# Eight shared 4 KB tiles as eight tags, handed out by the kernel, and another written order of tasks

## The chip, the cores and the metric

The kernel runs on one core of a Trainium2 chip. The metric is the time of one execution on the device, in microseconds (us), lower being better. The core has five engines that run side by side: TensorE (PE; its weight loads are listed as PEld), VectorE (DVE), ScalarE (ACT), GpSimd (POOL) and SyncE (SP), which here only starts transfers (DMAs). Each engine takes its instructions in the order in which the program gives them; semaphores between engines hold an instruction back until what it reads is there, or until a buffer that it writes is free.

## The reference

The reference is a DeltaNet attention (4 batches, 8 heads, 768 positions, head size 48) followed by a feed-forward layer with a cosine gate. Cut to what is computed:

```python
k_n = k / (norm(k) + 1e-06)
for t in range(S):                       # state: (B, H, D, D), zero at first
    y[:, :, t] = einsum('bhd,bhde->bhe', q[:, :, t], state)
    v_old = einsum('bhde,bhd->bhe', state, k_n[:, :, t])
    state = state + beta[t] * einsum('bhd,bhe->bhde', k_n[:, :, t], v[:, :, t] - v_old)
x = y.transpose(0, 2, 1, 3).reshape(3072, 384)
h = x @ w_in                             # (384, 2048)
out = (h * cos(h)) @ w_out               # (2048, 384)
```

## The kernel before

**Units and pairs.** The 768 positions are cut into 24 chunks of 32, the units n = 0 to 23, each for all 32 pairs of batch and head at once; two units make a pair m = n // 2. Within a unit the recurrence is solved as a triangular system, and between units a state is handed on, so the units follow each other.

**What a unit does.** SyncE loads its k, q and v (L308). In the first eight units TensorE turns k and q (task turn, L513) and ScalarE copies the result out (turn_out, L523). TensorE forms the products of keys and queries (gram, L544), and VectorE takes them out of PSUM as gram_keys (L555) and gram_queries (L578). The keys' norms come by way of square (ScalarE, L448), sum (VectorE, L453), norms (GpSimd, L465) and scale (VectorE, from L476). The two grams of a pair go to memory in the device (gram_put) and come back in another layout (gram_get, L609 and L617); the triangular matrix is inverted in pieces (inv, L654 and L661): on VectorE for pair 0, in four pieces, and on GpSimd for the others, in seven. The inverse goes out (put, L675) and comes back for each unit (get, L686 and L694). For unit 0 half of get's eight DMAs are started by ScalarE, the others by SyncE. Then TensorE runs state (L711), for units 0 and 1 solve_half, between (both L741) and solve (L774), for others solve alone, then update (L797) and within (L814). VectorE's right, between_out, solve_out (two instructions, L784) and update_out (L805) and ScalarE's half_out and within_out carry the values between them. The features (L833, L840) of two units are the 128-column input of the feed-forward layer of pair p.

**The feed-forward layer.** For p = 0 it is plain: hidden 0,f for eight even f (L884, three PSUM banks in turn), the gate as turns (ScalarE, L924), rest (VectorE, L931), cos (ScalarE, L940) and gate (VectorE, L943), and out 0,i,k (L1026). For p from 1 on the products are done by Strassen's scheme with seven products in place of eight (layer, L1001; the second matrix, L1083). Both weight matrices arrive as 64-bit words, in 28 loads of 512 KB (w_in, 0 to 11) or 384 KB (w_out, 12 to 27), each into a 4 KB tile (L413), and are narrowed by split (two instructions on ScalarE, L421 and L423), shift (two on VectorE, L427 and L432) and add (one on GpSimd, L436). The load is called weights t, and its steps split t, shift t and add t.

**What sets the order.** The work is a set of 1869 tasks, put in with `add` under names such as ("gram", 5), each with its dependencies and the tiles that it makes and uses. A text, `Order.LINE`, lists their indices in the order in which `run` emits them. Engines take their tasks in the order of that list; the tile framework puts in the semaphores. A task stands in the queue of its engine alone, so the list decides what is queued behind what.

**The shared tiles.** Eight tiles of 4 KB per partition have the tag "g". They hold, one after another, `bq`, `eye16` and `halves_z` (constants of the start), `t_beta`, the words of each weight load (`pairs`, free after add t), the squares of keys (`ksq`, free after sum), the half solutions of units 0 and 1 (`u_half`) and the gates (`g_ffn`, free after the last product that reads them). A task that makes such a tile waits, in its engine's queue, until the last user of the tile that it gets is done. PSUM gives one tile each to the tags "kq" and "two" (turned keys, grams, half solutions, updates, features), three to "h" and two halves to the output.

Of the kernel before, what the change touches and what calls it, by code (L numbers as in the profile page):

```python
# [10 lines left out]
FP = mybir.dt.float32  # L11
I32 = mybir.dt.int32
U32 = mybir.dt.uint32
# [3 lines left out]
C = 32  # L17
# [36 lines left out]
0 1 2 3 4 5 6 1757 72 10 37 14 11 7 12 42 38 1761 39 13 15 40 16 43 17 44 1758 18 45 46 19 75 73 20  # L54
48 1765 50 79 96 49 1769 97 47 76 1759 77 80 104 78 99 131 51 1762 81 105 52 53 54 1773 9 154 55
1777 82 100 56 1770 36 1766 1778 1763 1771 134 101 1760 102 106 107 1774 135 41 1781 1772 108 1767
83 136 22 1782 109 1783 23 1775 1764 132 84 1785 1779 21 1789 1784 110 1793 1786 1768 1780 1776 24
25 1787 185 111 26 27 1797 28 29 137 57 1801 30 32 31 1790 33 138 58 155 139 34 74 1788 35 112 1805
140 59 669 1794 1798 141 670 142 60 674 113 1791 1802 1806 61 1803 114 186 62 1799 143 63 115 1809
64 65 66 68 208 1813 671 116 67 98 158 1817 675 676 69 1804 86 239 677 117 1795 188 672 159 1792  # L60
1818 160 118 103 1814 161 1810 1821 87 119 679 162 1800 678 70 680 1819 133 681 1815 163 189 673
1825 1796 71 1811 192 684 682 1822 1823 85 1820 1807 683 1826 193 689 1816 190 164 1827 690 694 165
691 685 8 1808 1812 692 191 1824 1829 88 262 686 709 89 1828 90 166 92 693 1830 687 93 695 721 167
688 91 696 697 699 1833 1834 1831 94 704 156 95 194 168 700 1837 1835 121 157 120 195 698 196 1841
812 701 122 1832 241 705 702 1836 1838 1842 197 737 123 706 703 124 707 209 1845 169 293 242 742 125
708 738 739 722 1846 126 1843 1839 127 128 1849 710 170 129 743 740 130 1844 744 1840 187 747 171
741 745 752 212 1850 1847 172 1853 316 1851 746 748 1848 1857 757 213 749 753 754 214 755 750 1858
245 145 1854 756 762 751 173 215 1852 758 146 808 1855 759 763 216 1861 760 1859 217 711 1862 764
767 1856 1863 144 1860 243 1865 265 147 1864 761 1866 148 725 218 768 772 149 1867 1868 151 769 770
246 295 219 771 220 152 150 174 729 153 244 726 730 712 713 221 175 715 210 176 222 177 211 247 223  # L70
716 178 733 179 180 347 181 714 266 182 717 773 248 183 765 774 199 809 775 810 723 184 776 249 250
718 200 267 268 736 224 811 719 269 777 781 296 780 817 766 240 734 819 783 778 818 782 731 816 820
271 225 832 720 784 813 251 821 727 822 724 299 779 226 227 272 786 823 833 788 825 789 826 319 735
790 824 273 834 827 835 829 791 792 785 297 794 728 298 828 830 270 198 201 840 836 841 796 787 274
300 837 797 842 843 814 838 798 831 202 203 301 844 845 846 799 205 848 800 847 370 206 839 850 795
849 204 793 275 229 852 230 228 851 231 854 863 853 801 320 232 276 233 235 856 864 321 802 277 804
207 732 263 880 855 349 857 865 805 236 278 279 234 815 302 806 858 859 353 303 294 867 237 803 304
879 860 317 868 869 866 238 322 807 280 253 871 882 264 870 323 872 873 874 861 911 862 910 281 912
305 913 324 325 875 885 886 876 914 915 877 878 252 881 254 327 917 916 326 926 888 883 354 887 927
928 401 884 890 919 920 350 918 255 351 891 256 929 921 923 934 922 892 893 930 924 935 931 352 932  # L80
257 374 259 894 896 258 328 373 282 260 936 933 925 898 424 938 897 937 283 939 942 940 284 943 944
946 329 355 895 375 889 330 941 285 899 900 286 947 287 948 945 331 950 957 901 332 951 261 958 288
902 949 356 289 333 290 952 903 904 959 960 357 954 953 961 974 965 906 334 455 407 907 966 358 962
291 955 963 905 908 376 967 964 307 968 318 973 292 976 308 335 1005 956 979 359 980 408 306 969
1006 1004 403 970 1007 478 975 404 377 378 971 1009 972 309 982 409 310 1008 311 313 1020 405 379
909 977 428 984 336 380 978 312 985 381 1010 1021 986 314 987 337 988 990 1022 338 992 1011 993 1013
1014 1023 981 1012 406 1015 1016 1017 994 339 315 1028 1024 1029 340 983 995 1018 1019 382 1025 1026
989 1027 509 462 427 1030 341 348 1031 1032 383 996 342 384 997 1033 1036 998 991 1038 1034 1037 410
343 1068 1040 1000 411 344 1001 1039 385 1051 1052 457 1041 1053 1035 412 1042 386 1002 1043 1054
1067 1044 1046 1045 387 413 345 1047 461 999 429 1055 346 1070 1073 1048 1049 1059 1056 1060 1050  # L90
1061 1062 430 1057 361 1063 371 1099 1058 431 1064 1100 388 1003 1065 1098 1074 482 1101 1071 402
1103 1066 372 389 362 1102 433 1069 1076 360 1104 1105 1078 1079 1107 1072 1106 1114 1115 390 1077
435 1080 434 432 1116 1109 1081 363 1082 1084 364 458 463 365 367 1117 366 1108 1086 1111 436 1087
368 437 1122 1085 1088 532 1075 481 1123 1083 1110 1124 1118 1089 1125 1112 459 1119 391 1120 1090
1130 1121 369 425 392 393 1131 1113 1126 394 460 1127 438 456 1132 395 1091 396 516 1134 1128 1129
479 515 464 426 397 1092 1133 1136 398 439 440 1145 441 399 1135 1094 1095 1093 1137 1146 465 1096
466 1138 1140 1147 1161 400 1139 1141 1148 1142 563 1149 1097 1143 1164 1162 1150 442 480 1151 1152
1163 1153 1144 1167 1157 483 1193 1168 484 1158 415 1192 1159 1160 443 467 1170 1154 485 1155 1156
1172 1194 1195 1173 486 1196 487 1165 1197 1166 517 1199 414 511 1198 1208 416 586 536 1200 1174
1201 417 1175 1176 1178 418 1203 488 1169 512 1209 1180 513 1202 1204 1181 1212 489 1210 1182 1205  # L100
1213 419 490 1214 1171 421 570 1211 1216 1217 1183 1215 1206 1218 420 444 1219 514 535 422 1184 1224
1207 491 1225 1220 1177 1226 1227 1221 1228 1179 565 445 1185 1222 1223 423 446 447 1230 1186 492
448 537 1188 1189 1239 1229 1240 1231 617 493 1241 449 451 452 566 1232 1233 1190 1234 1236 1235 450
510 1256 1242 1243 1247 1255 1258 1237 569 518 469 1244 1248 1245 453 1246 1238 1187 454 590 1191
1249 494 1251 1261 1250 1262 1287 519 1252 1253 1288 1289 1286 1259 520 1254 470 1290 538 539 1302
1264 495 496 1291 567 1257 497 541 1260 1292 1293 1266 540 1295 1303 1294 521 1267 1296 1297 1304
1263 1298 571 1268 1306 1299 1305 1307 468 543 1308 1269 542 471 1270 1309 544 1272 640 1300 1318
472 498 533 1310 473 1311 1301 1265 545 589 475 1274 474 1312 1313 1314 1271 1275 546 476 623 619
1276 499 1277 1320 477 1319 1315 1278 500 1316 591 501 1279 1273 502 568 503 1317 547 504 564 1322
548 624 1280 1324 1321 1333 1323 534 1334 572 505 1282 1326 573 1350 1325 506 507 1283 1328 1327 574  # L110
1284 1329 1281 575 1330 549 592 1337 1335 1336 523 1331 1349 593 1341 508 1338 1342 620 550 1343
1339 1352 1340 1344 1332 1381 551 1355 1345 1346 595 643 1382 1356 621 1347 1383 1380 524 1385 522
1348 1353 1351 1387 1358 1386 1389 1384 622 1390 1388 1396 1360 594 587 1391 1354 1397 1361 525 1398
597 1393 526 527 1399 596 529 598 1392 1404 599 530 1405 1406 600 528 1400 1407 1362 1285 1394 1395
1363 601 553 1364 1357 1366 1412 625 1408 602 644 1359 1401 1368 1409 1402 552 1410 554 1369 1370
1411 618 531 555 1414 556 1413 1371 1403 1415 1416 1372 1418 557 645 1373 558 1367 1417 626 1419
1374 1427 559 1420 1365 627 560 1376 1428 1422 641 1429 628 603 1421 1377 1430 561 604 1375 1424 642
1378 562 1423 605 1443 1425 588 1431 1432 1426 1439 1446 1433 646 1440 1441 577 1434 1449 1442 1475
1379 1450 1435 1436 1476 1474 1452 647 1437 1438 648 1477 1447 1479 576 1481 1480 1454 1483 1444 578
1478 649 651 1445 1448 629 1451 1482 1484 1455 579 1456 580 1485 581 583 650 1457 1486 1458 1490  # L120
1494 1495 1491 582 652 584 1496 1460 1492 1493 1487 1498 607 1499 1497 585 1462 608 606 1488 1489
1461 1463 1459 1464 1502 1465 653 609 1466 1453 1506 1503 1504 654 1500 610 611 655 1501 613 1507
1467 1508 1468 1505 614 1510 1512 1470 1509 1521 1511 1522 1523 1471 612 1514 1515 1513 1524 1516
# [1454 lines left out]
```

## Time and profile before

| | |
|---|---|
| three runs | 670.10, 670.51, 671.60 us; median 670.51 |
| profiled execution | 673.52 us, of which the span of its instructions is 671.7 |
| mean granted clock of TensorE | 0.959 |
| busy: PE, DVE, ACT, POOL | 607.6, 466.9, 223.6, 343.5 us |
| share of the span | 90%, 70%, 33%, 51% |
| moved by DMA | 59.65 MB, mean 89 GB/s |

All times that carry a position ("at 88.3 us") count from the start of the span of the profiled execution. "Busy" is the time in which an engine works on instructions that the profile counts. "Idle before" is the time in which an engine stood still ahead of an instruction, and the releaser is the instruction or DMA whose end let it go on; where the profile finds none, it writes "issue". The granted clock is TensorE's, as a share of its full speed. The chain of waits follows the work back from the last instruction to whatever released it.

### The profile page before, as it was taken

What the parts mean: (1) busy time and instruction counts of PE and PEld (TensorE: products, weight loads), DVE (VectorE), ACT (ScalarE), POOL (GpSimd) and SP (SyncE); (2) the same over time, 40 slices, a digit from 0 to 9 for tenths busy, and PEclk for the clock granted to TensorE, in tenths of its full rate; (3) what the DMA queues carried; (4) which work ended last, traced back from release to release, by engine and by line L of the source; (5) the groups of instructions that cost most, each with busy time, mean ns of one, the idle gap of its engine ahead of it and who ended that gap; (6) DMA issues with size and microseconds to landing.
All of it is one profiled execution on the core that took longest, in us unless ns stands there. A gap on an engine that the chain in (4) does not pass through costs nothing.

```text
span 671.7 us, 27640 instructions
## 1 busy us (share of the span) xinstructions
PE 607.6 (90%) x12060; PEld 571.4 (85%) x12060; DVE 466.9 (70%) x912; ACT 223.6 (33%) x376; POOL 343.5 (51%) x734
## 2 busy tenths in 40 slices
PE   3326669999899999999999999999999999999997
PEld 3215668886698999999999999999989999999997
DVE  6783548856887786858777877768776766656662
ACT  3342255543132332323423333333322324323330
POOL 4278748876878358318448358368284084000000
PEclk9556969999999999999999999999999999999999
DMA  7886564475464553554555354454623213001001
GB/s 164 200 193 153 115 148 103 99 147 99 83 113 79 106 94 62 90 98 69 113 93 96 68 96 81 74 85 94 112 47 79 55 23 87 6 21 53 1 13 35
DMA packets 237084, 59.65 MB, mean 89 GB/s; under 512 B 228516, under 2 KB 231860, under 8 KB 236964
## 3 DMA queue, kind: packets, MB, share of 16 engines
q1 hardware_dynamic: 233956, 57.03, 42.9%
q8 instruction: 94, 1.54, 1.0%
q10 hardware_dynamic: 2752, 0.43, 0.4%
q0 software_dynamic: 256, 0.44, 0.3%
q14 instruction: 26, 0.21, 0.1%
HBM read 43.17 MB, written 14.68 MB: 86 GB/s over the span
## 4 chain that ended last, share of the span: by engine, by line
PE 83%; DMA 4%; DVE 3%; issue 3%; POOL 3%; SPq 3%; ACT 1%; ACTq 0%; DVEq 0%; POOLq 0%
PE p_h L1001 29%; PE p_out L1083 29%; PE p_h L884 6%; PE p_kq L711 4%; PE p_s L797 3%; PE p_u L774 3%; PE p_kq L814 3%; PE p_out L1026 2%; PE p_g L544 2%; PE p_o L1083 2%; SPq L308 1%; DMA qp<-in_q_dram 1%; POOL knrm L465 1%; DMA x_ffn<-y_dr 1%; POOL z L661 1%
## 5 line engine op out<-in xcount | busy, mean ns | idle before, releaser
L654 POOL TENSOR_TENSOR part<-z,gb 128x126 f32<-128x126 f32 (+22 forms) x341 | 133.2, 391 | 107.9 <-DMA gb<-g_dr 52.6
L661 POOL TENSOR_TENSOR z<-z,part 128x126 f32<-128x126 f32 (+22 forms) x341 | 137.7, 404 | 26.7
L1001 PE MATMUL p_h<-x_ffn,w_in 128*128 128x128 f32 x1120 | 143.2, 276 | 0.7 <-issue 0.7
L1001 PEld LDWEIGHTS p_h<-x_ffn,w_in 128*128 128x128 f32 x1120 | 135.4, 192 | 1.9 <-issue 0.9
L1083 PE MATMUL p_out<-w_out,g_ffn 128*128 128x192 f32 x672 | 122.1, 329 | 0.0
L924 ACT ACTIVATE turns<-p_h,quarter_turn 128x512 int32<-128x512 f32 x96 | 65.2, 685 | 149.6 <-DVE p_h L1019 101.0
L1083 PEld LDWEIGHTS p_out<-w_out,g_ffn 128*128 128x128 f32 x672 | 107.7, 190 | 1.5
L940 ACT ACTIVATE turns<-turns,halfpi 128x512 f32<-128x512 f32 x96 | 68.0, 720 | 90.7 <-DVE turns L931 90.3
L1083 PE MATMUL p_out<-w_sum,g_ffn 128*128 128x192 f32 x496 | 88.7, 329 | 0.0
L931 DVE SCALAR_TENSOR_TENSOR turns<-p_h,turns 128x512 f32<-128x512 f32 x96 | 65.1, 682 | 28.6 <-ACT turns L924 28.3
L1083 PEld LDWEIGHTS p_out<-w_sum,g_ffn 128*128 128x128 f32 x496 | 79.7, 190 | 1.0
L943 DVE TENSOR_TENSOR g_ffn<-turns,p_h 128x512 f32<-128x512 f32 x96 | 64.7, 679 | 14.4 <-ACT turns L940 12.1
L465 POOL TENSOR_TENSOR knrm<-ksum,halves 128x16 f32<-128x16 f32 (+1 forms) x14 | 36.4, 2605 | 64.2 <-DVE ksum L453 52.7
L1016 ACT COPY g_ffn<-p_h 128x512 f32<-128x512 f32 x60 | 34.9, 582 | 97.3 <-PE p_h L1001 97.2
L1099 DVE TENSOR_TENSOR g_ffn<-g_ffn 128x512 f32<-128x512 f32 x88 | 61.5, 708 | 1.7 <-PE p_out L1083 1.6
L1019 DVE TENSOR_TENSOR p_h<-g_ffn,p_h 128x512 f32<-128x512 f32 x60 | 41.4, 691 | 30.2 <-PE p_h L1001 24.1
L884 PE MATMUL p_h<-x_ffn,w_in 128*128 128x128 f32 x384 | 48.5, 286 | 1.2 <-DVE g_ffn L943 0.8
L1133 DVE SCALAR_TENSOR_TENSOR o<-p_out,o 128x192 f32<-128x192 f32 x74 | 25.1, 351 | 33.8 <-PE p_out L1083 30.3
L884 PEld LDWEIGHTS p_h<-x_ffn,w_in 128*128 128x128 f32 x384 | 46.5, 200 | 2.3 <-DVE g_ffn L943 0.9
L1001 PE MATMUL p_h<-x_sum,in_sum 128*128 128x128 f32 x320 | 41.6, 277 | 0.0
L784 DVE TENSOR_TENSOR u<-p_u,bz 128x384 f32<-128x384 f32 x48 | 24.4, 549 | 21.8 <-PE p_u L774 21.8
L1001 PEld LDWEIGHTS p_h<-x_sum,in_sum 128*128 128x128 f32 x320 | 38.8, 192 | 0.6
(111 smaller groups left out, 728.9 us busy)
## 6 DMA issues: line engine op xcount, KB each, us to landing
pairs<-in_moe_w_in_dram SPq DMA_DIRECT2D x12, 512.0 KB
pairs<-in_moe_w_out_dram SPq DMA_DIRECT2D x16, 384.0 KB
gb<-g_dr SPq DMA_DIRECT2D x22, 256.0 KB
vp<-in_v_dram SPq DMA_DIRECT2D x96, 48.0 KB
out_dram<-o SPq DMA_DIRECT2D x23, 192.0 KB
y_dr<-y SPq DMA_DIRECT2D x20, 192.0 KB
x_ffn<-y_dr SPq DMA_DIRECT2D x40, 96.0 KB
kp<-in_k_dram SPq DMA_DIRECT2D x128, 24.0 KB
```

The costliest lines, as they stand in the source:

```text
L465: nc.gpsimd.tensor_tensor(out=scales[m][2][:, part], in0=sums[m, part.start][:, 0:n], in1=halves[:, 0:n], op=ALU.pow,)
L654: eng.tensor_tensor(out=part, in0=z[:, 0:rows, j, None].to_broadcast(shape), in1=a[:, j, None, j + 1 :].to_broadcast(shape), op=ALU.mult,)
L661: eng.tensor_tensor(out=behind, in0=behind, in1=part, op=ALU.subtract)
L884: nc.tensor.matmul(p_h[:, i], w_in[:, t, (4 * k + i) * 128 : (4 * k + i + 1) * 128], moved(p, t, unit), start=(t == 0), stop=(t == KT - 1),)
L924: nc.scalar.activation(turns[p, f], hidden_of(p, f), AF.Identity, bias=quarter_turn, scale=TURN)
L931: nc.vector.scalar_tensor_tensor(out=r, in0=hidden_of(p, f), scalar=TURN, in1=t, op0=ALU.mult, op1=ALU.subtract,)
L940: nc.scalar.activation(r, r, AF.Sin, bias=halfpi, scale=2.0 * math.pi)
L943: nc.vector.tensor_tensor(out=place(p, f), in0=step_of(rests.pop((p, f)), f), in1=step_of(hidden_of(p, f), f), op=ALU.mult,)
L1001: nc.tensor.matmul(p_h[:, e], in_sum[:, odd_tile, 4 * s + e] if a == "s" else w_in[:, a, f * 128 : (f + 1) * 128], x_sums[p][:, unit] if b ...
L1019: nc.vector.tensor_tensor(out=block(p, s, 0, 1) if i == 3 else p_h, in0=block(p, s, *one), in1=p_h, op=ALU.add,)
L1083: nc.tensor.matmul(p_o, left(p, part, a)[:, e % 4], right(e, b), start=(e == 0), stop=(e == FT // 2 - 1), skip_group_check=True,)
L1099: nc.vector.tensor_tensor(out=left(p, s, to), in0=left(p, s, one), in1=left(p, s, two), op=op)
```

## The change

The tag "g" of eight tiles becomes eight tags g0 to g7 of one tile each. `run` keeps a list of the free ones: a task that makes such a tile takes the first of that list, and the tag comes back at its end when the last user of the tile has been emitted. So the choice of the tile is made by the written list and not by the framework. The three constants take g0, g1 and g2. As a gate tile must be taken by the task that makes it, gate (p, f) for f = 2, 6, 10, 14 now also depends on gate (p, f - 2). The list `LINE` is a new one throughout: the same 1869 tasks, in another order.

```diff
     LINE = """
-0 1 2 3 4 5 6 1757 72 10 37 14 11 7 12 42 38 1761 39 13 15 40 16 43 17 44 1758 18 45 46 19 75 73 20
...
+0 1 2 3 4 5 6 1757 10 72 14 11 12 7 42 15 73 37 38 1761 39 13 16 43 75 17 1758 1762 40 18 76 44 45
...
     def run(self, wrote):
         keys, done = list(self.tasks), set()
         live, left = dict.fromkeys(self.bufs, 0), dict(self.users)
+        homes, free = {}, [f"g{i}" for i in range(self.bufs["g"])]
...
-            for tag, _ in makes:
+            for tag, t in makes:
                 live[tag] += 1
                 assert live[tag] <= self.bufs[tag], key
+                if tag == "g":
+                    self.home = homes[t] = free.pop(0)
             emit()
...
                 if left[t] == 0:
                     live[self.tiles[t]] -= 1
+                    if t in homes:
+                        free.append(homes[t])
...
-    bq = ffn_pool.tile([128, NU, C], FP, name="bq", tag="g", bufs=GATES)
+    bq = ffn_pool.tile([128, NU, C], FP, name="bq", tag="g0", bufs=1)
...
-        pairs = ffn_pool.tile([128, 4, TOK], U32, name="pairs", tag="g", bufs=GATES)
+        pairs = ffn_pool.tile([128, 4, TOK], U32, name="pairs", tag=order.home, bufs=1)
...
-            [128, 2, H, D], FP, name="ksq", tag="g", bufs=GATES
+            [128, 2, H, D], FP, name="ksq", tag=order.home, bufs=1
...
-        add(("gate", *key), "DVE", 0.73, lambda: hidden_gate(p, f), [("cos", *key)],
+        deps = [("cos", *key)]
+        if f in range(2, FT, 4):
+            deps.append(("gate", p, f - 2))
+        add(("gate", *key), "DVE", 0.73, lambda: hidden_gate(p, f), deps,
             makes=makes, uses=uses + [("turns", *key)], due=due)
```

The same replacement of the tag is made for `eye16`, `halves_z`, `t_beta`, `u_half` and `g_ffn`. Around the steps that the prediction speaks of, the new list stands against the old one so:

| engine | before | after |
|---|---|---|
| SP | weights 4, v 0, k 5, weights 5, put 0, v 1, weights 6, gram_put 3, q 4, gram_put 2, weights 7, get 0 | weights 4, k 5, weights 5, v 0, put 0, weights 6, gram_put 2, gram_put 3, v 1, weights 7, get 0 |
| ACT, early | inv_out 0, split 3, 2, 5, square 2,0, split 4, 6, half of get 0, split 7, half_out 0 | split 4, 3, inv_out 0, split 5, 2, square 2,0, split 7, half of get 0, split 6, half_out 0 |
| ACT, later | half_out 1, turns 0,2, within_out 1, cos 0,2, square 3,0, cos 0,0, turn_out 5 | turns 0,0, square 3,0, split 11, half_out 1, turns 0,2, turn_out 5, split 12, within_out 1, cos 0,0 |
| PE | update 1, within 1, turn 5, state 2, gram 5, hidden 0,4, features 1, turn 6, hidden 0,6, 0,8, 0,10, solve 2, out 0,0,0 | update 1, turn 5, within 1, gram 5, hidden 0,4, features 1, state 2, hidden 0,6, 0,8, turn 6, out 0,0,0, hidden 0,10, solve 2 |
| POOL | inv 1,4, add 11, inv 1,5, add 8, inv 1,6, add 10, add 9, add 15 | inv 1,2, add 8, inv 1,3, add 10, inv 1,4, add 9, inv 1,5, inv 1,6, add 11, add 15 |

## The prediction, made before the changed kernel ran

> **What bounds the kernel now.** I read the page's rows of busy tenths and of the granted clock first, then TensorE's waits before and after 100 us, then the chain of waits, and last the timelines of ScalarE, GpSimd and VectorE around the longest wait. From the page, the 40 slices (16.8 us each):
>
> ```profile
> PE   3326669999899999999999999999999999999997
> ...
> PEclk9556969999999999999999999999999999999999
> ```
>
> TensorE is 90% busy over the span, and from the seventh slice on nearly all the time. A new order can gain only in the first 180 us. There, of the first 100 us, are these waits of TensorE (engine, line, what it waited for: total, times, longest):
>
> ```profile
> PE p_w L741 <- DMA halves_z<-z_dr: 16.1, 1, 16.1
> ...
> PE p_g L544 <- ACT kq_t L523: 4.7, 1, 4.7
> ...
> PE p_kq L711 <- issue: 2.3, 1, 2.3
> ...
> PE p_t L513 <- ACT x_ffn L840: 0.8, 1, 0.8
> ```
>
> I summed all of TensorE's idle stretches over 0.25 us: 59.2 us, of which 41.2 lie before 76 us (loads, and the inverse of pair 0 that must come back through get 0), 10.1 between 76 and 109 us, 4.2 more up to 180 us, and 3.7 in single "issue" gaps after it. After 180 us no task waits for another engine: nothing is to be had there, only lost.
>
> The 4.7 us row is the wait of gram 5, at 83.61 to 88.34 us. The chain of waits shows how it came about (start, us, engine, operation):
>
> ```profile
> 84.57 1.29 POOL w_in L436
> ...
> 85.88 0.84 ACT ksq L448
> 86.72 0.61 ACT turns L940
> 87.33 0.96 ACT kq_t L523 x2
> ...
> 88.34 1.18 PE p_g L544 x61
> 89.53 5.43 PE p_h L884 x24
> ```
>
> ScalarE stood still in front of square 3,0 (its timeline):
>
> ```profile
> 85.88 0.84 ACT L448 ACTIVATE ksq<-kp 128x768 f32<-128x768 f32 x1 [5.82 <-POOL w_in L436]
> ```
>
> Square 3,0 needed a 4 KB tile, and the one it got was that of load 10, whose last user is add 10; add 10 stands on GpSimd behind the last piece of inverse 1 (78.37 to 84.61). Behind square 3,0 on ScalarE stood turn_out 5, for which gram 5 waited. The windows (us, then busy of PE, PEld, DVE, ACT, POOL, the granted clock, DMA share, GB/s) show what followed:
>
> ```profile
> 80.00:85.00 5.00, 1.35 (x128) 1.08 (x109) 0.93 (x1) 0.06 (x1) 4.14 (x13) 0.96 0.51 122
> 85.00:90.00 5.00, 1.66 (x66) 1.49 (x67) 0.44 (x2) 4.12 (x9) 2.09 (x2) 0.50 0.64 133
> 90.00:95.00 5.00, 5.00 (x26) 5.00 (x25) 2.12 (x5) 0.97 (x4) 1.01 (x1) 0.52 0.78 160
> ```
>
> The granted clock fell to half from 84.58 to 94.82 us, and hidden 0,4, which takes 2.85 to 2.95 us at full clock, took 5.49.
>
> **The change, part by part.** *Homes.* Eight tags of one tile in place of one tag of eight: no instruction is added. A tile now waits for the one tile whose last user stands earliest in the list among those free. By itself that is worth about 0: in the trace the tiles were handed out nearly in that order already. The added dependency of a gate on the gate two before it holds in both lists. What counts is the new list.
>
> *Start to 66 us: -0.5 us (-2 to +2).* Solve_half 0 waits 16.12 us for get 0, whose last DMA landed at 45.92. The inverse of pair 0 on VectorE carries scale 1,0 between its pieces now (five small instructions, 1.0 us) and ends about 31.3 us, not 29.9. Put 0 stands on SyncE behind loads k 5, weights 5 and v 0, where before v 0 came earlier; v 1 has moved behind weights 6 and two gram_puts. The four DMAs of q 4 no longer stand between put 0 and get 0. Against that: get 0 has half of its DMAs on ScalarE, now behind both instructions of split 7, which wait for weights 7. Issued about 36.8 us by the shorter queue, and with the 4.0 to 4.1 us that weights 5, 6 and 7 took to land, weights 7 is there at 41; that half is then issued at 41 to 43.5 and lands 1.5 to 2.5 us later (its rows), at 43 to 45. SyncE's half landed at 45.2 to 45.9, so it stays the later one, slightly earlier than before. If weights 7 isn't issued until after v 1's four DMAs, as late as before (41.04), its split ends at 46.5 and solve_half 0 comes 2 us late: the upper end. Behind it on ScalarE waits half_out 0, which needs solve_half 0 anyway.
>
> *76 to 109 us: -6.0 us (-7.7 to -4).* On ScalarE, turn_out 5 now stands behind square 3,0, as before, but square 3,0 comes earlier and its tile is that of load 6, whose add 6 ended long before 66 us; on GpSimd, add 10 has moved three pieces of inverse 1 ahead. So gram 5 no longer waits: -4.73. TensorE's list is now update 1, turn 5, within 1, gram 5, hidden 0,4, state 2, and so on, so matmuls fill 78 to 95 us and the clock should hold: hidden 0,4 takes 2.9 instead of 5.49, -2.6. The wait of turn 6 for features_out 1 (0.81) goes, for hidden 0,6 and 0,8 come before it. Removed: 8.1 us.
>
> Added: turn 5 needs the bank that update_out 1 gives back, right behind update 1: about 1.1 us, between the hand-overs of the same bank in this chain (0.74 and 0.75 ahead of solve 0 and 1, 0.93 ahead of between 0, 1.24 ahead of update 1). TensorE's whole queue stands behind it. Features 1 needs a bank from gram_queries 5, which stands on VectorE behind shift 12 and 14: 0.35 (two instructions of 0.55 and 0.35 there, less 0.5 of cover by hidden 0,4). Hidden 0,6 waits for gate 0,0 (one of three banks), and 0,8 for gate 0,2 behind features_out 1 and shift 13: 0.25 and 0.4. Sum 2.1; 8.1 - 2.1 = 6.0. The 2.26 us "issue" gap in state 2 has no releaser in the trace; I leave it where it is (if it came of the idle time, -1.7 more: the lower end). As a check, the list up to out 0,0,0 and hidden 0,10 holds the same matmuls in both; before it ends at 108.1, and durations at full clock added up along the new list with these waits end it at 101.8. Inverse 1 has add 8, 10 and 9 ahead of its last piece (before: 11 and 8), some 1.3 us more, so put 1 goes out at about 86 and get 2 lands, 12 us after put 1's issue as in the trace (84.64 to 96.73), at 98; solve 2 comes at 101: 3 us of cover.
>
> *109 to 180 us: -0.8 us (-1.5 to +0.5).* Update 5's wait of 1.53 goes (solve_out 5 stood behind weigh 3 and turn_out 8 on VectorE; weigh 3 is far later now). Update 2 gets 0.7, behind shift 18 and gate 0,8.
>
> *After 180 us: +1.2 us (0 to +4).* Two places. Six pairs of solve and update now have only one half product (1.31 us) between them, to cover solve_out's two instructions (2 x 0.549): a spare of 0.29 each, and VectorE finds something ahead of it about as often as not; 0.5 in all. And the loop of pair 8: gram_put 17 to solve 16 took 60.6 us in the trace (376.6 to 438.1 with gram 17's end), with 58.8 us of TensorE's work beside it. The new list has 48.6 us there. But gram_get 8 has moved up on SyncE, no longer behind get 14, k 21 and blocks 19,1, and get 16 stands right behind put 8: I shorten the loop by 10.7 us, to 49.9, and count 0.7.
>
> Sum: -0.5 - 6.0 - 0.8 + 1.2 = -6.1. The profiled execution took 673.52 (span 671.7 and 1.8 around it), so 667.4; the median of the three runs is 3.0 lower, 670.51, so **664.4 us**. With the stages' ends, not all at once, 660.5 to 667.
>
> **Rivals.** *The clock falls all the same (0.13): 668.* VectorE's chain over 82 to 92 us is dense now (shifts, gates, rests), and it runs beside GpSimd's adds. The same shift took (VectorE's timeline)
>
> ```profile
> 40.17 1.51 DVE L432 TENSOR_SCALAR w_in<-w_in 128x512 uint32<-128x512 uint32 x1
> ...
> 42.54 0.41 DVE L432 TENSOR_SCALAR w_in<-w_in 128x512 uint32<-128x512 uint32 x1
> ```
>
> the first beside an add, the second alone. Three such stretches ahead of gate 0,0 and 0,2 cost 3 x 1.1 = 3.3 us, for which hidden 0,6 and 0,8 wait; with a little of the half-clock time (2.6 at most) I take 3.5, and of the 6 us 2.5 are left. For it: the rows. Against it: of GpSimd's adds, 15, 12, 14 and 13 wait for shifts of this stretch, and 8, 9 and 10 are done by then. [...]
>
> *Nothing changes (0.08): 670.5.* The tiles come in the old order, square 3,0 waits for another late user, and the chain moves with it. The list speaks against it: add 6 stands a long way ahead.
>
> *Slower (0.17): 674.* The loop of pair 8 doesn't shrink. GpSimd's inverse 8 (396.2 to 424.5) is the same 28.3 us, so all must come from the time between gram_put 17 and inverse 8, 12 us of queueing and transfer in the trace. If it stays 12, solve 16 waits 60.6 - 48.6 = 12 us less what little else is brought forward, about 10: 664.4 - 0.7 + 10 = 674. It decides from half: once that stretch stays over 6 us, the gain at 76 to 109 us is spent. For it: the list gives the loop 10 us less of TensorE's work than before. Against it: the order on SyncE.
>
> **How the numbers follow.** The forecast has 0.62, the rivals 0.13, 0.08 and 0.17. What the measurement can tell from no change is about 0.2%, 1.3 us. Faster: 0.59 of the forecast and 0.10 of the clock's rival, 0.69. Same: 0.02, 0.02 and 0.06, 0.10. Slower: 0.21. The range of 660 to 672 takes in the forecast's own, the clock and no change, and leaves out the loop's case and the lowest ends, about 0.2.
>
> **What would show it.** ScalarE has no wait for an add ahead of square 3,0; gram 5 starts about 81 and not at 88.3; the clock stays 1.0 over 80 to 95 us; hidden 0,6 starts about 89 and not at 97.0; solve_half 0 starts between 44 and 46; update 5 has no wait. I'm wrong if TensorE has a wait of several us for get 16 near 430 us, for get 0 after 46, or for gates at 85 to 95.

## The result, and the profile after

The changed kernel takes 674.38 us (median of nine runs, 672.64 to 678.86 without one disturbed run of 684.0), the kernel before on the same chip 671.22. The ratio is 1.0056, with a 95% interval of 1.0030 to 1.0082: **0.56% slower**, where 664.4 us and 1% faster had been forecast, and outside the range. The profiled execution took 678.22 us (span 676.4), 4 us more than the median; a second profiled execution (the first experiment) took 675.52.

From the page of the changed kernel, the same two rows as of before:

```profile
PE   3308789989999899999999999999999999999996
PEclk9756899999989999999999998999999999999999
```

The stretch from 84 to 101 us (sixth slice) is 8 tenths busy where it had been 6. New are the 8s far behind, at slices 12 and 25 of the clock. The waits of TensorE (line, what it waited for, total, times, longest), in the kernel before behind 100 us:

```profile
PE p_kq L711 <- issue: 3.4, 3, 1.4
PE p_s L797 <- DVE u L784: 1.5, 1, 1.5
PE p_u L774 <- issue: 1.0, 1, 1.0
PE p_h L884 <- DVE g_ffn L943: 0.8, 1, 0.8
```

and in the changed kernel, first up to 76 us, then behind 100 us:

```profile
PE p_w L746 <- DMA halves_z<-z_dr: 24.1, 3, 23.0
```

```profile
PE p_kq L716 <- issue: 3.0, 2, 2.2
PE p_u L779 <- DMA zt<-z_dr: 2.6, 5, 1.1
PE p_out L1088 <- DVE g_ffn L1104: 2.4, 1, 2.4
PE p_h L889 <- DVE g_ffn L948: 1.6, 1, 1.6
PE p_out L1088 <- issue: 1.5, 1, 1.5
```

Gram 5's 4.7 us are gone, as forecast. In their place stand a longer wait for get 0 (23.0 and 0.9 instead of 16.1) and, behind 100 us, new waits for the gets of later units (tile zt, 2.6 us) and, by its row, for VectorE's L1104 (2.4 us). Waits put down to "issue" stand in both kernels, at other tasks. The windows show the gain itself:

```profile
80.00:85.00 5.00, 5.00 (x150) 4.46 (x149) 1.80 (x5) 4.47 (x10) 4.14 (x11) 0.74 0.49 119
85.00:90.00 5.00, 3.91 (x150) 3.49 (x149) 4.40 (x7) 3.01 (x6) 4.00 (x7) 1.00 0.84 152
90.00:95.00 5.00, 3.03 (x26) 2.76 (x25) 3.54 (x5) 2.40 (x5) 5.00 (x4) 1.00 0.53 87
```

TensorE works 11.94 us of these 15 (8.01 before), and the clock is 1.0 in two windows of three.

The most useful table is one of lags: wherever both lists have issued the same set of TensorE's tasks, the end of the last in the changed kernel less that in the kernel before (profiled executions).

| after the task | ends, changed | lag | what happened since the row above |
|---|---|---|---|
| gram 3 | 24.99 | -4.24 | k 3 and q 3 land earlier |
| solve_half 0 | 51.42 | +3.98 | get 0 later |
| update 1 | 77.70 | +0.56 | the "issue" gap of 2.91 in solve 0 is gone |
| within 2 | 108.65 | -5.24 | gram 5 doesn't wait |
| state 6 | 172.02 | -6.88 | waits of before are gone, solve 4 waits |
| out 1,3,0 | 191.02 | -6.01 | |
| out 1,3,1 | 199.16 | -1.76 | solve 6 waits 1.5 for get 6, half clock 195.2 to 198.7 |
| out 2,0,1 | 231.14 | -0.73 | state 8, "issue" 2.21 |
| within 14 | 399.63 | +0.06 | state 12, "issue" 0.77, and others |
| layer 6,1,3 | 417.70 | +4.36 | 2.36 ahead of out 5,6,0, half clock 406.9 to 410.3 |
| layer 9,1,6 | 567.30 | +4.36 | out 8,3,1, "issue" 1.48; state 19's 1.43 of before gone |

The gain came, 5 to 7 us, and more than all of it was lost behind 190 us, where the prediction had put 1.2.

### The profile page after: what moved, and what is told of

The parts are those of the page before. It is cut to its first block, busy times and chain, and to the rows that moved or that the text cites. A ratio compares the mean times of both kernels' runs of the same rounds, so it can differ in the third digit from the quotient of the medians.

```text
span 676.4 us, 27648 instructions
## 1 busy us (share of the span) xinstructions
PE 610.8 (90%) x12060; PEld 572.7 (85%) x12060; DVE 467.4 (69%) x912; ACT 224.2 (33%) x376; POOL 350.4 (52%) x734
## 3 DMA queue, kind: packets, MB, share of 16 engines
q8 instruction: 95, 1.56, 1.0%
## 4 chain that ended last, share of the span: by engine, by line
PE 69%; DMA 8%; POOL 8%; SPq 7%; DVE 3%; issue 3%; ACT 1%; ACTq 0%; DVEq 0%; POOLq 0%
PE p_h L1006 27%; PE p_out L1088 26%; SPq L313 4%; POOL z L666 4%; PE p_kq L716 3%; POOL part L659 3%; PE p_u L779 2%; DMA gb<-g_dr 2%; PE p_s L802 2%; PE p_kq L819 2%; DMA kp<-in_k_dram 2%; PE p_g L549 2%; PE p_o L1088 2%; PE p_h L889 1%; DMA pairs<-in_moe_w_in_dram 1%
## 5 line engine op out<-in xcount | busy, mean ns | idle before, releaser
L666 POOL TENSOR_TENSOR z<-z,part 128x126 f32<-128x126 f32 (+22 forms) x341 | 142.6, 418 | 26.7
L1006 PEld LDWEIGHTS p_h<-x_ffn,w_in 128*128 128x128 f32 x1120 | 135.0, 192 | 1.4 <-DVE g_ffn L1024 0.2
L1088 PE MATMUL p_out<-w_sum,g_ffn 128*128 128x192 f32 x496 | 90.9, 332 | 1.9 <-issue 1.5
L948 DVE TENSOR_TENSOR g_ffn<-turns,p_h 128x512 f32<-128x512 f32 x96 | 64.8, 678 | 21.2 <-ACT turns L945 18.0
L1104 DVE TENSOR_TENSOR g_ffn<-g_ffn 128x512 f32<-128x512 f32 x88 | 61.6, 705 | 1.0 <-PE p_out L1088 0.5
L889 PEld LDWEIGHTS p_h<-x_ffn,w_in 128*128 128x128 f32 x384 | 44.2, 192 | 7.1 <-issue 3.4
```

The source lines that it names most:

```text
L666: eng.tensor_tensor(out=behind, in0=behind, in1=part, op=ALU.subtract)
L889: nc.tensor.matmul(p_h[:, i], w_in[:, t, (4 * k + i) * 128 : (4 * k + i + 1) * 128], moved(p, t, unit), start=(t == 0), stop=(t == KT - 1),)
L948: nc.vector.tensor_tensor(out=place(p, f), in0=step_of(rests.pop((p, f)), f), in1=step_of(hidden_of(p, f), f), op=ALU.mult,)
L1006: nc.tensor.matmul(p_h[:, e], in_sum[:, odd_tile, 4 * s + e] if a == "s" else w_in[:, a, f * 128 : (f + 1) * 128], x_sums[p][:, unit] if b ...
L1088: nc.tensor.matmul(p_o, left(p, part, a)[:, e % 4], right(e, b), start=(e == 0), stop=(e == FT // 2 - 1), skip_group_check=True,)
L1104: nc.vector.tensor_tensor(out=left(p, s, to), in0=left(p, s, one), in1=left(p, s, two), op=op)
```

## The experiments

Sixteen kernels ran. "Homes" are the eight tags handed out by the list. Edits of the list are shown by the names of tasks. Each ratio is to the kernel before on the same chip.

**1. The changed kernel again, and the two halves of the change apart.** No edit for the first; for the second the new `LINE` in the old program; for the third the old `LINE` in the new one, with

```diff
-        if f in range(2, FT, 4):
-            deps.append(("gate", p, f - 2))
...
-                   [("g", ("gates", p, f // 4 % 2, f // 8))] if f % 4 == 0 else [],
+                   [("g", ("gates", p, f // 4 % 2, f // 8))]
+                   if (p, f) in ((0, 2), (1, 6)) or f % 4 == 0 and (p, f) not in ((0, 0), (1, 4)) else [],
```

> The changed kernel once more, unaltered, to see which of its waits come back in another profiled execution. Theory (the gain at 76 to 109 us is real and is given back later, at solve 4 and 6, which wait for get 4 and get 6, and at out 5,6,0, which waits for left 5,3,1): median 673 to 675; in the profile solve_half 0 starts at 47 to 49 us, TensorE waits again for get 6 near 194 us and for left 5,3,1 near 407 us. Rival (these waits are chance of the one execution, and something steady, as the tiles' tags, costs 3 us): the median is the same, and the waits at 194 and 407 are gone or under 0.5 us.

> The new list with the old shared tag g of eight tiles. Theory (the list makes the difference, the hand-out of tiles by tags does nothing): as the changed kernel, 673 to 675. Rival (the tags cost): 671 or less.

> The old list with the eight tags handed out by the list. Two gate tiles are taken by the other gate of their tile, as the old list has gates 0,2 and 1,6 ahead of 0,0 and 1,4. Theory (the list alone): as the kernel before within 0.2%, 670 to 672.5. Rival (the tags cost): 673.5 to 675.

| | shared tag | homes |
|---|---|---|
| old list | 672.01 | 665.59, ratio 0.9911 (0.9878 to 0.9944) |
| new list | 674.10, ratio 1.0038 (1.0013 to 1.0063) | 674.98, ratio 1.0044 (1.0020 to 1.0067) |

The third was a surprise against both theories: homes gain 6 us, but only with the old list. With the new list they are worth nothing that shows. Taken in this order, the change has two parts of opposite sign: **the hand-out -0.9%, and the list on top of it +1.3%**. Taken the other way round, the list alone costs 0.4% and the hand-out then does nothing: in the profiles either of the two ends the 4.7 us wait of gram 5. ScalarE's timeline of the third kernel shows where its gain comes from:

```profile
79.44 0.48 ACT L830 COPY y<-p_kq 128x384 f32<-128x384 f32 x1 [5.98 <-PE p_kq L819]
79.82 0.73 ACT L945 ACTIVATE turns<-turns,halfpi 128x512 f32<-128x512 f32 x1
80.44 0.83 ACT L453 ACTIVATE ksq<-kp 128x768 f32<-128x768 f32 x1
81.18 0.71 ACT L945 ACTIVATE turns<-turns,halfpi 128x512 f32<-128x512 f32 x1
81.79 0.57 ACT L528 COPY kq_t<-p_t 128x512 f32<-128x512 f32 x1
```

Square 3,0 (L453) has no wait: by the list it gets the tile of load 11, and add 11 stands two pieces of inverse 1 ahead of add 10. The framework had given load 11's tile to weights 14, a load with time to spare (in the kernel before it was issued at 73.35 us, 0.03 us after add 11's end). The lag of the third kernel to the kernel before is -7.3 us at update 2 and -9.6 at the end, and behind 100 us no task waits for a get.

In the second execution of the changed kernel the same waits came back: 23.03 us ahead of solve_half 0, 0.93 for get 6, and the gaps of the table further down.

**2. Get 0's late half.**

```diff
-weights 7, split 7, add 5, norms 2,0, get 0, weights 8
+weights 7, get 0, split 7, add 5, norms 2,0, weights 8
```

> The changed kernel with get 0 one place earlier in the list, so that its half on ScalarE stands ahead of split 7 and no longer waits for weights 7; SyncE's order is unchanged. Both theories: solve_half 0 starts near 44 instead of 48 us. Theory (from 100 us on GpSimd's inverse of the next pair, its way out and back sets the time, so what TensorE gains earlier it loses at solve 2): solve 2 waits 3 to 4 us for get 2, and the median is 673 to 675 as before the edit. Rival (TensorE's time simply adds up): 4 us less, 669 to 671.

It took 672.02, ratio 1.0001 (0.9983 to 1.0020): 3 us less than the changed kernel beside it, between the two theories. Solve_half 0 started at 43.41, 4.4 us earlier than in the changed kernel beside it. Solve 2 did not wait for get 2; the theory with GpSimd's loop was wrong there, though solve 6 waited 0.6 us for get 6. Part of it was lost at once (TensorE's waits of 40 to 110 us):

```profile
PE p_w L746 <- DMA halves_z<-z_dr: 17.9, 2, 17.5
PE p_u L779 <- DVE u_half L764: 2.8, 2, 2.1
...
PE p_h L889 <- issue: 2.1, 1, 2.1
PE p_h L889 <- POOL w_in L441: 1.7, 1, 1.7
```

Between_out 0 stood behind shift 6 and 7 on VectorE (2.1). The last row puts 1.7 us in hidden 0,0 down to add 8, but hidden 0,0 needs adds 0 to 2 alone, and add 8 narrows other columns. By its place in the stream this is a gap of the kind told under 5.

**3. Which part of the list.** The new list up to within 2 and the old one for the rest, and the other way round, both with homes.

> Homes, with the new list up to within 2 (some 110 us) and the old list for the rest. Old list throughout with homes took 665.6, new list throughout 675. Theory (most of what the new list costs is behind 110 us: waits for get 6, instruction loads at state 8, left 5,3,1): 666 to 669. Rival (the early part, with turn 5 ahead of within 1 and get 0's half behind split 7, costs it): 671 to 675.

> Homes, with the old list up to within 2 and the new list for the rest. Theory (the cost is behind 110 us): 670 to 674, with waits again for get 6, at state 8 and for left 5,3,1. Rival (the cost is in the early part): 665 to 668.

New then old: 668.04, ratio 0.9932 (0.9906 to 0.9959). Old then new: 674.78, ratio 1.0059 (1.0033 to 1.0085). So the cost of the list lies behind 110 us, nearly all of it; by the two ratios with the old list behind 110 us (0.9932 and 0.9911) the early part costs 1.4 us, and their intervals overlap.

**4. One task moved in the kernel before.** Shared tag, old list:

```diff
-inv 1,5, add 8, inv 1,6, add 10, add 9
+inv 1,5, add 8, add 10, inv 1,6, add 9
```

> The kernel before, shared tag and old list, with one task moved: add 10 stands ahead of the last piece of inverse 1 on GpSimd. Theory (what the homes give with the old list, 6.4 us, is the one wait of square 3,0 for add 10 and what follows from it): square 3,0 has no wait for add 10, gram 5 starts near 82 us, the clock stays at 1.0 from 85 to 95 us, and the median is 665 to 667. Rival (the homes gain by other hand-outs as well): 668 to 671. Second rival (the inverse of pair 3 takes the gain back, so that solve 6 waits): 669 to 672, with a wait for get 6 near 195 us.

It took 668.09, ratio 0.9934 (0.9911 to 0.9956), in the range of the first rival. Its ScalarE has no wait ahead of square 3,0 (81.51), gram 5 ends at 86.14 and not 89.53, and no get is waited for. The clock fell all the same, from 86.0 to 89.4, and gram 5 started at 85.28 and not near 82: state 2 ahead of it has an "issue" gap of 2.54 us, where the third kernel has one of 0.42. So that one wait is most of what homes give with the old list; whether 0.9911 and 0.9934 differ the intervals leave open.

**5. Left 5,3,1.** The row above puts 2.4 us on VectorE's L1104, which is left 5,3,1, so it was moved ahead.

```diff
-right 15, layer_out 6,1,0, gate 6,(0,0,1), ..., left 5,3,1
+left 5,3,1, right 15, layer_out 6,1,0, gate 6,(0,0,1), ...
```

> The changed kernel with left 5,3,1 moved ahead of right 15 on VectorE, so that out 5,6,0 need not wait for state 15, right 15 and a gate. Theory (the waits of the new list late in the kernel add up, as TensorE alone sets the time there): the 2.1 to 2.4 us wait near 405 us goes, and the half clock behind it where there was one; median 1.5 to 4 us below the changed kernel on the same chip, 671 to 673. Rival (another engine's chain is the bound there and takes the time back): as the changed kernel within 1 us, with a wait of the same size elsewhere behind 405 us.

It took 675.06, ratio 1.0056 (1.0036 to 1.0075): nothing. VectorE and TensorE of this kernel:

```profile
400.95 0.68 DVE L1104 TENSOR_TENSOR g_ffn<-g_ffn 128x512 f32<-128x512 f32 x1
```

```profile
401.06 1.38 PE L716 MATMUL p_kq<-st,kq_t 48*32 48x48 f32 x128
404.77 1.49 PE L1088 MATMUL p_out<-w_out,g_ffn 128*128 128x192 f32 x4 [2.34 <-issue]
```

Left 5,3,1 ends at 401.63, and out 5,6,0 starts at 404.77 all the same, now with "issue" in the place of a releaser. The attribution had been wrong: in the list, out 5,6,0 stands ahead of left 5,3,1, so it cannot need it, and in the changed kernel's profile it starts 0.5 us after left's end, too late for a hand-over (others take 0.05 to 0.15). In the second execution of the changed kernel it started 0.13 us after it: there the time alone would not have told.

That sent me to the rows with "issue". The page lists a DMA queue of instructions:

```profile
q8 instruction: 95, 1.56, 1.0%
```

The trace has each of its 95 packets at 16 KB. The 24,120 matmul and weight-load records of TensorE and the 158 instructions of its sequencer are 24,278: the 1.56 MB shared out over them are 64 bytes each, 256 to a packet. So I took this queue for TensorE's program, 256 instructions to a load, an estimate by size alone so far. In the profiles of all the kernels told here, before and after too, TensorE has 115 gaps over 0.5 us without a releaser, and every one of them ends 1.2 to 1.8 us after the end of a packet of this queue, though such a packet comes only every 7 us. At out 5,6,0 it was 1.3 to 1.5 us in each of eight executions (404.57 to 405.74 for the gap of 404.77 to 407.13; 402.25 to 403.25 for that of 402.44 to 404.77). A state is 128 matmul records and 128 weight loads: one whole load in 1.4 us.

The place in the stream says it most plainly. Number all of TensorE's instructions of a profile from 0 in the order of their starts (matmuls, weight loads and the sequencer's). Then all 115 gaps, the eight ahead of out 5,6,0 and the one in hidden 0,0 under 2 stand at number 193 or 194 modulo 256: TensorE makes these stops at one place in every 256 instructions alone, as it would at the crossing from one load into the next. Most crossings have no stop: the changed kernel's 95 loads have five over 0.5 us, out 5,6,0's among them.

| gap ahead of or in | hidden 0,6 | state 8 | state 12 | out 5,6,0 | out 8,3,1 |
|---|---|---|---|---|---|
| changed kernel | 1.29 | 2.21 | 0.77 | 2.36 | 1.48 |
| again | 1.47 | 2.90 | 0.98 | 2.08 | 1.75 |
| new list, shared tag | 1.30 | 2.62 | 1.29 | 2.33 | 1.14 |
| old to within 2, then new | - | 2.48 | 1.32 | 1.78 | 0.61 |

These are the new list's own; the old list has others, 1.43 in state 19 and 0.6 to 1.3 in five more places behind 100 us (the kernel before). Behind some of them the granted clock falls to half, for 3.4 us (406.9 to 410.3 in the changed kernel) or 6.8 (217.8 to 224.6 with get 0 moved). In the kernel of the last row these gaps and one of 2.58 in state 13 come to 8.8 us behind 100 us, against 3.2 with homes and the old list, and 6.8 us at half clock (216.1 to 223.0) cost up to 3.4 more. Together that is up to 9.0 of the 9.1 us between the two profiled executions; the gets are waited for only 0.3 us there.

**6. State 8 parted from gram 11.** In the new list state 8 follows gram 11 at once, and gram 10 and within 7 are close ahead:

```diff
-gram 11, gram_put 10, features_out 7, state 8, ..., layer 2,1,6, ..., layer 2,1,7
+gram 11, gram_put 10, features_out 7, ..., layer 2,1,6, ..., layer 2,1,7, state 8
```

> The changed kernel with state 8 moved behind layer 2,1,6 and 2,1,7, so that it no longer follows gram 11 at once. Theory (TensorE's gaps without a releaser are waits for its own instructions, which come in loads of 16 KB, and a run of tasks of short matmuls uses them up faster than they come): the gap of 2.5 to 2.9 us in state 8 shrinks below 1 us and the half clock behind it (220 to 227 us) goes; 670 to 672.5, 3 to 5 us below the changed kernel. Rival (the gap belongs to the load and the place in the instruction stream, and so stays wherever state 8 stands): a gap of 2 to 3 us again, within the layers or state 8, and 674 to 676.

It took 669.22, ratio 0.9972 (0.9949 to 0.9995), some 5 us less than the changed kernel (1.0044 to 1.0056), and a little below the theory's range. The second execution of the changed kernel and this one, windows:

```profile
216.00:224.00 8.00, 5.07 (x212) 4.71 (x211) 3.99 (x8) 1.49 (x3) 6.59 (x19) 0.91 0.61 119
224.00:230.00 6.00, 6.00 (x40) 6.00 (x40) 2.67 (x5) 2.19 (x5) 1.34 (x6) 0.84 0.62 90
```

```profile
216.00:224.00 8.00, 8.00 (x241) 7.58 (x240) 6.59 (x12) 3.49 (x6) 6.59 (x19) 1.00 0.63 123
224.00:230.00 6.00, 6.00 (x44) 6.00 (x44) 4.30 (x10) 1.71 (x4) 2.02 (x7) 1.00 0.59 86
```

TensorE is busy all 8 us instead of 5.07, and the clock stays at 1.0 (0.91 and 0.84 there). Lag to that execution behind state 8: -4.26, for a gap of 2.90; the rest is the half clock. The same crossing still falls into state 8, but now the long matmuls of the layers stand ahead of it, and there is no stop.

**7. The stream shifted.** To tell the order from the place in the loads, gram 3 was repeated in a stretch in which TensorE waits for get 0 anyway; the repeats give the same result. Three times over with the new list and with homes and the old list:

```diff
-        for j in range(NP):
+        for j in list(range(NP)) * (3 if n == 3 else 1):
```

> The changed kernel with the 32 matmuls of gram 3 done three times over (same operands, same result; 64 matmuls and 64 weight loads more), in a stretch in which TensorE waits 23 us for get 0, so that they cost nothing there. All later instructions of TensorE shift by 128 in its stream, half of a load of 16 KB, if one instruction takes 64 bytes (1.54 MB over some 24,000 instructions). Theory (the gaps are waits for instructions, and where they fall hangs on the place in the stream): the gaps at state 8, state 12, out 5,6,0 and out 8,3,1 change place and size; the median moves by 1 to 5 us, to either side. Rival (the gaps belong to the tasks and the order around them): same gaps at the same tasks, and 674 to 676.

> Homes with the old list (665.6), and the same 64 additional matmuls in gram 3. Theory: its gaps (0.7 in state 14, 1.4 in state 19, 1.1 in layer 10,1,1) change place and size, and the median moves by up to 4 us, rather upward, as its gaps are few: 665 to 670. Rival: 665 to 666.5, same gaps.

673.51 (ratio 1.0043, 1.0014 to 1.0073) and 666.87 (0.9937, 0.9912 to 0.9962), and the new list's gaps at the same tasks (1.80, 2.48, 1.36, 2.36, none at out 8,3,1). That looked like the rival, but I had miscounted: a gram leaves 64 matmul records, not 32, so two repeats are 256 instructions, a whole load. The runs shifted nothing and could not tell. With one repeat, half a load:

```diff
-        for j in range(NP):
+        for j in list(range(NP)) * (2 if n == 3 else 1):
```

> The changed kernel with gram 3 done twice: by the trace's count (64 matmul records and 64 weight loads for one gram's 32 products) 128 instructions more, 8 KB, half of one 16 KB load; three times over was a whole load and shifted nothing. Theory (where a gap falls hangs on how a run of short matmuls lies to the loads): the gaps at state 8, state 12, out 5,6,0 and out 8,3,1 change by over 1 us each in at least two places, the loads near them come at other tasks, and the median moves by 1 to 5 us, to either side. Rival (the run of short matmuls alone decides): the same gaps within 0.7 us, 673 to 676.

> Homes with the old list, and gram 3 done twice, half a load more. Theory (the place to the loads decides): its gaps at state 14, state 19 and layer 10,1,1 go and others come, and the median moves by 1 to 4 us. Rival: as without, 664 to 667.

**700.49** (ratio 1.0430, 1.0404 to 1.0456) and **699.69** (1.0446, 1.0397 to 1.0494). Half the added work of the runs that cost nothing, and 26 to 34 us more, whatever the list. The theories had 1 to 5 and 1 to 4. The half-shifted new list, TensorE's waits behind 100 us:

```profile
PE p_kq L716 <- issue: 17.7, 8, 2.7
PE p_g L549 <- issue: 2.3, 1, 2.3
PE p_u L779 <- issue: 2.2, 3, 0.8
```

and one of them in the timeline, state 4:

```profile
138.33 1.21 PE L716 MATMUL p_kq<-st,kq_t 48*32 48x48 f32 x109
142.28 0.32 PE L716 MATMUL p_kq<-st,kq_t 48*32 48x48 f32 x17 [2.74 <-issue]
142.54 1.75 PE L889 MATMUL p_h<-x_ffn,w_in 128*128 128x128 f32 x9
```

Nearly every even state now stops in its second half, for 1.7 to 2.7 us (p_kq rows: 17.7 us in 8 stops; 21.2 in 10, up to 3.1, with the old list, states 3 and 5 among them, against 2.1 in 2 without the shift), and the clock falls behind most of them (mean granted clock 0.947 and 0.946 in the profiled executions). So it matters where the crossings lie. Counted in matmul and weight-load records from the start, modulo 256, states 10, 16, 18 and 20 of the old list begin at 24 or 248, and at 152 or 120 when shifted. A state is one load long, so each has one crossing: in the old list it comes after 18 to 65 of the 128 matmul records of an even state, in the shifted one after 89 to 126 of each state that stops. There most of the 256 instructions ahead of the crossing are the state's own, used up in about 1.4 us.

The place alone does not decide. States 5, 7 and 22 of the half-shifted new list have their crossing after 105 to 118 records and do not stop, and without the shift state 8 stops after 48, while states 6 and 10 of the same list pass theirs after 51 and 42, a gram directly ahead of all three. What tells state 8 from them (gram 10 and within 7 close ahead, perhaps) was not tested apart, nor was how much other transfers delay the loads.

**8. State 15, and all three places.** State 8 as above, and

```diff
-layer 6,1,0, ..., state 15, ..., out 5,6,0, right 15, ..., solve 15, out 5,6,1
+layer 6,1,0, ..., out 5,6,0, state 15, right 15, ..., out 5,6,1, solve 15
```

> The changed kernel with state 8 behind layer 2,1,6 and 2,1,7, and state 15 behind out 5,6,0 (solve 15 behind out 5,6,1). Theory (the 2.1 to 2.4 us in front of out 5,6,0, which the profile puts down to left 5,3,1, is a wait for TensorE's instructions, used up by state 15 right after update 14 and within 14): the wait shrinks below 1 us and there is no half clock behind it; 665 to 668, 2 to 4 us below the kernel with state 8 alone (669.2). Rival (a true wait for VectorE or for the place in the stream): a gap of 2 us again near 402 us, and 668 to 670.

> The same, and get 0 ahead of split 7. Theory (what the new list costs against the old one is these three places, instructions at state 8 and 15 and get 0's late half): 662 to 665.5, as the old list with homes (665.6) or better. Rival (the rest of the new list costs as well, at 76 to 110 us and at solve 6): 666 to 670.

The first: 667.98 where the kernel before took 668.82 on this chip, ratio 0.9987 (0.9966 to 1.0007), no gain on state 8 alone (0.9972). The gap ahead of out 5,6,0 is gone, but a true wait took its place at out 5,6,1, which does need left 5,3,1. VectorE of this kernel:

```profile
398.34 0.55 DVE L731 TENSOR_TENSOR rhs<-vp,p_kq 128x384 f32<-128x384 f32 x1 [2.97 <-PE p_kq L716]
398.81 0.68 DVE L948 TENSOR_TENSOR g_ffn<-turns,p_h 128x512 f32<-128x512 f32 x1
399.41 0.85 DVE L1104 TENSOR_TENSOR g_ffn<-g_ffn 128x512 f32<-128x512 f32 x1
```

Left 5,3,1 stands behind right 15 and a gate, right 15 waits for state 15, and out 5,6,1 starts 0.06 us after left's end (400.32): this is how a real hand-over looks. Left ahead of right 15 and state 15 later, together, was not tried. The second: 664.50, ratio 0.9945 (0.9924 to 0.9965). Against 1.0044 to 1.0056 for the changed kernel, the three places are 1%. But get 0 earlier is no part of what the new list costs behind it, and the kernel under 9 (0.9880), with get 0 early and the old list from there on, is the fair measure: against it the new list still costs 0.65%, some 4 us, and these two intervals are apart. In the profiles the lag between the two grows by 3.9 us between within 14 and within 15, where out 5,6,1 waits 1.85 us for left 5,3,1 and the clock falls from 396.6 to 400.1.

**9. The best of both.** Homes, the new list up to solve_half 0 with get 0 ahead of split 7, the old list for the rest.

> Homes, the new list up to solve_half 0 with get 0 ahead of split 7, and the old list for the rest. Theory (TensorE's time adds up where GpSimd's inverses don't bind): solve_half 0 starts near 43 instead of 46.4 us, and the median is 661 to 665. Rival (the inverse of pair 1, whose start the move doesn't bring forward, gives the pace from there): 665 to 668.

It took 662.98 (four runs), ratio 0.9880 (0.9863 to 0.9896), the fastest of all and 1.2% below the kernel before. Solve_half 0 starts at 42.58 (46.38 with homes and the old list); the lag to homes with the old list is -5.3 us at solve 0 and -2.6 to -3.5 from turn 6 to the end.

## Why the prediction was wrong, point by point

**"By itself [the hand-out] is worth about 0: in the trace the tiles were handed out nearly in that order already."** With the old list this is wrong: the hand-out is worth -0.89%, 6 us. "Nearly" hid the one tile that mattered: square 3,0 got load 10's tile where the list's order gives it load 11's. I compared tiles only for the new list, where a new order had moved add 10 too, and credited the list alone with a gain that either of the two brings. With the new list the hand-out is worth nothing (674.10 and 674.98), so this is not the step that missed the total.

**"The added dependency of a gate ... holds in both lists"**: wrong. The old list has gate 0,2 ahead of gate 0,0 and gate 1,6 ahead of 1,4. Two gate tiles had to be taken by the other gate for the old list to run with homes.

**Start to 66 us, -0.5.** SyncE's half of get 0 landed at 42.95, 3 us earlier than before, as worked out. ScalarE's half was issued at 42.16 to 43.52 by weights 7 (landed 42.13), near what I had, but it took 5.4 to 6.6 us to land and not 1.5 to 2.5: large loads issued at 40.9 to 43.4 (weights 8, two of gram_get 1, weights 9) were in flight. So solve_half 0 ended 4 us late, and the sign that I had named, a wait for get 0 after 46, came. I had named the row, but took its duration from an emptier moment (165 GB/s over 39 to 44 us in the kernel before; 42 to 47 us has 233 here). That the stage ended only 1.1 us off (+0.56) was luck: the gap of 2.91 us in solve 0, one of the stops at a crossing, fell away.

**76 to 109 us, -6.0.** This term held: -5.8 (lag +0.56 to -5.24). Turn 5 cost 1.13 (1.1 forecast), hidden 0,6's gate 1.09 (0.25), features_out 1 0.68. The clock fell once, for 3.4 us from 79.2. That the number is so near is in part luck: the clock's fall, the dearer gate and a new stop of 1.29 in hidden 0,6 were made up for by the stop of 2.26 in state 2, which went. And all of this gain, and 2.5 us more by within 2, comes with the old list and homes as well.

**109 to 180 us, -0.8**: -1.6 by the lags. Update 5's wait went.

**After 180 us, +1.2 (0 to +4).** This is the step that failed and turned the sign: +11.2 in the profiled execution (lag -6.88 to +4.36), and +9.3 in the second (-8.46 to +0.85). Of these, in the first and the second execution, 2.3 and 4.7 us came at state 8 and 4.3 and 2.5 at out 5,6,0, both of them stops at a crossing; 4.2 and 2.1 came at solve 6, behind get 6. "After 180 us no task waits for another engine: nothing is to be had there, only lost" was right, but I treated the "issue" gaps as fixed things without a cause ("I leave it where it is") and looked for the loss in GpSimd's loop alone. By what stands under 5 (each 1.2 to 1.8 us behind a packet of the instruction queue, each at one place in 256) they are waits for TensorE's own instructions; their place hangs on the order of TensorE's tasks, and a new order deals them anew. Counting the records between two loads would have shown into which tasks the crossings fall, though not which of them stop.

**The rivals.** The slower one had the sign and nearly the time (674), by luck, for its mechanism was not the main one: get 16 was not waited for. A piece of it was seen at pair 3, where TensorE, 6 us ahead, waited 1.5 us for get 6 in one execution and 0.9 in another, with half clock behind it in the first; with homes and the old list, 10 us ahead, it did not wait at all. GpSimd's inverse of that pair ended at 186.04 in the changed kernel and at 181.45 there; why was not looked into. The clock's rival did not occur where I put it; half clock came behind the gaps instead and made 2.4 us into 4. "Nothing changes" is what homes do with the new list.

**The clock.** The prediction had it hold once gram 5's wait of 4.73 us is gone and matmuls fill the stretch. The runs show falls behind much shorter stops: 2.36 us ahead of out 5,6,0, and 1.5 us in two pieces at solve 6. A gap of 1.43 us in state 19 of the kernel before left the clock at 1.0, but the same gap with the old list and gram 3 three times over was followed by half clock (484.1 to 487.5), and one of 2.62 in state 8 (new list, shared tag) was not. So the length of a stop alone does not say whether the clock falls.

## What to carry to other kernels

When a hand-out of buffers and an order change together, work out each with the other held fixed: here -0.9% and +1.3% looked like one small loss, and half of the change with the old order was better than either kernel. In a kernel bound by TensorE, take rows with "issue" seriously: count its instructions against the loads of its instruction queue (16 KB each here), part tasks of many short matmuls by longer ones where a stop falls into them, and shift the stream by half a load with harmless repeats in an idle stretch to see how much hangs on it. And before a releaser is believed, look whether the task needs it at all, at the time between its end and the start it is said to have allowed, and at the place of the wait in the stream.

## What the runs showed of the hardware

By the count under 5, TensorE's instructions come in loads of 16 KB, 256 instructions each (95 loads for 24,278 in the changed kernel), and their arrival is not always hidden: with nearly the same work, a shift by half a load moved the time by 26 to 34 us (4% to 5%). Behind most loads no gap is seen (five over 0.5 us for those 95), but states, 256 instructions in 1.4 us, stopped for up to 3.1 us, always at number 193 or 194 modulo 256. Half clock behind such a stop made it cost more than itself: 2.90 us in state 8 cost 4.26.
